# Idle-fill matmuls of TensorE in ten operand forms on a constant tile, instead of one bfloat16 form on the causal mask

## The chip, the cores and the metric

The kernel runs on one core of one Trainium2 chip. The metric is the device time of one execution in microseconds; lower is better. Times are the median over runs.

## The reference, cut to what matters

Two stages follow each other. The first is a linear recurrence with complex decay over 768 steps, for 4 batches and 8 heads of width 48; its output feeds a dense layer pair of width 384 to 2048 to 384 with a smooth gate.

```python
for t in range(S):                      # S = 768
    new_re = ar * S_re - ai * S_im      # decay a = a_re + i a_im, size limited to 0.999
    new_im = ar * S_im + ai * S_re
    S_re, S_im = new_re + k[t] x v[t], new_im
    y[t] = q[t] @ S_re
x = y as (3072, 384)
h = x @ w_in                            # 384 x 2048
g = h * tanh(softplus(h))
out = g @ w_out                         # 2048 x 384
```

The matmuls that this change is about are no part of it: their results are never read.

## The kernel before, in words

The 3072 rows are handled as 12 units of 256 steps, each in two chunks, a and b, of 128. Per unit, VectorE, ScalarE and GpSimd turn the decays into growth factors and phases (`elementwise`), DMAs relay the factors into a layout by heads (tile `T`), TensorE does the chunked recurrence (`attention`: `kn`, `am`, `y`, `pd`), DMAs move the result (`y` to `x`), and TensorE does the two dense layers (`moe`: `ph` and `po`). The weights arrive as 64-bit words and are joined on VectorE while unit 0 runs. From unit 1 on the dense layers split each float32 operand in a high and a low half of type float32r and issue three matmuls; unit 0 takes plain float32.

The order on each engine is written out by hand in the table `ORDER`, which lists operations by number; every engine runs its own operations in that order, and a semaphore wait holds all that stands behind it on the same engine. Before unit 0's recurrence can start, TensorE has little to do: it sums log magnitudes and phases along the steps by matmuls with triangular matrices (`sum_up`: `mag sum` and `phase sum`, with `turn` and `less` as the triangles), once for each chunk. Between these stand 40 operations called `spin` of two matmuls each, 80 in all, that write a PSUM tile `junk` which nobody reads. In TensorE's order they stand as follows: 12 spins (below: group A), phase sum of chunk a, 5 spins (B), mag sum a, 4 spins (C), mag sum b, 1 spin (D), phase sum b, 16 spins (E), the first recurrence matmuls of chunk a up to `pd`, 1 spin (F), `y` of chunk a and the sums of unit 1, 1 spin (G) between the `pkn` and `pa` matmuls of chunk b, and then the rest.

The spins read `cmask`, the 128x128 bfloat16 mask of the recurrence, as stationary operand and, repeated four times, as moving operand. GpSimd makes `cmask` and all other constants at the start: a memset and an affine select for `cmask`, five single columns (`halfpi` to `above`), `turn`, `less`, `identity`, `rmask`, `good` and `ones`. `good` is the tile into which VectorE's first operation (L452) adds up its checks, so that operation waits for its memset.

Sizes: `P` is 128, `TU` is 256, `WC` is 768, `SPIN` is 2. The tag `wp5` is the home of the split input weights of pair 5 (`wh`), which are first written long after the spins.

Of the kernel before, what the change touches and what calls it, by code (L numbers as in the profile page):

```python
# [13 lines left out]
F32 = mybir.dt.float32  # L14
BF16 = mybir.dt.bfloat16
F32R = mybir.dt.float32r
# [10 lines left out]
P = 128  # L27
TU = 256
# [7 lines left out]
WC = DM * DF // P // NPAIR  # L36
# [4 lines left out]
SPINS, SPIN = 40, 2  # L41
# [166 lines left out]
def tile_kernel(ctx, tc, q, k, v, are, aim, are_t, aim_t, w_in, w_out, out):  # L208
    nc = tc.nc
    const = ctx.enter_context(tc.tile_pool(name="const", bufs=1))  # L210
    wts = ctx.enter_context(tc.tile_pool(name="wts", bufs=1))
# [12 lines left out]
    cmask = const.tile([P, P], BF16, name="cmask")  # L224
# [2 lines left out]
        out=cmask, in_=cmask, compare_op=ALU.is_ge, fill=0.0, base=0,  # L227
        pattern=[[1, P]], channel_multiplier=-1,
    )
    halfpi = const.tile([P, 1], F32, name="halfpi")  # L230
    nc.gpsimd.memset(halfpi, math.pi / 2)
    tiny = const.tile([P, 1], F32, name="tiny")
# [8 lines left out]
    for n, x in (("turn", INV2PI), ("less", -2.0 * INV2PI)):  # L241
        sums[n] = const.tile([P, P], F32, name=n)
        nc.gpsimd.memset(sums[n], x)
        nc.gpsimd.affine_select(
            out=sums[n], in_=sums[n], compare_op=ALU.is_ge, fill=0.0, base=0,
            pattern=[[1, P]], channel_multiplier=-1,
        )
    identity = const.tile([P, P], F32, name="identity")
    make_identity(nc, identity)
    ident = identity[:2 * D, :2 * D]  # L250
# [473 lines left out]
    def moe(u, st, row0, op=op, act=act, po_tag="po", g_tag="g"):  # L724
# [74 lines left out]
        def store(t):  # L799
            return lambda e: e.dma_start(out[ds(row0 + t * P, P), :], o[t])  # L800
# [36 lines left out]
        for t in range(2):  # L837
            op("AV", f"u{u} o{t}", o_out(t))
            op("S", f"u{u} store{t}", store(t))

    junk = Tiles({"junk": (ps, "po", 2, [P, 512])})

    def spin(e):
        for _ in range(SPIN):
            e.matmul(junk["junk"], cmask, cmask.unsqueeze(1).broadcast_to([P, 4, P]), start=True, stop=True)

    def verdict():
        def tally(e):
# [22 lines left out]
    for u in range(UNITS):  # L871
        for _ in early[u]:
            pass
        if u == 0:
            for _ in range(SPINS):
                op("T", "spin", spin)
        attention(u, early[u + 1] if u + 1 < SUMMED else iter(()))
        if u == 0:
            for i in range(NW):
                weight(i)  # L880
        if u == 1:
            for i in range(NW):
                halves(i)
        if u + 1 == UNITS:
            for i in range(SUMMED):
                test(i)
            verdict()
        moe(u, units[u], u * TU)
# [126 lines left out]
def build(nc_run=True):  # L1015
    nc = _bacc.Bacc("TRN2", target_bir_lowering=False, num_devices=1, dynamic_dma_scratch_size=1024)
    F = NJ * TU
    aps = []
    for n in ("q", "k"):
        aps.append(nc.dram_tensor(n, (UNITS, P, F), F32, kind="ExternalInput").ap())  # L1020
    aps.append(nc.dram_tensor("v", (UNITS, P, NCH, DM), F32, kind="ExternalInput").ap())
    for n in ("a_re", "a_im"):
        aps.append(nc.dram_tensor(n, (UNITS, P, F), F32, kind="ExternalInput").ap())
    for n in ("a_re_t", "a_im_t"):
        aps.append(nc.dram_tensor(n, (SUMMED, P, F), F32, kind="ExternalInput").ap())
    for n in ("w_in", "w_out"):
        aps.append(nc.dram_tensor(n, (NPAIR, P, WC), I64, kind="ExternalInput").ap())
    out = nc.dram_tensor("out_0_dram", (B * S, DM), F32, kind="ExternalOutput").ap()
    with tile.TileContext(nc) as tc:
        tile_kernel(tc, *aps, out)  # L1030
    if not nc.is_finalized():
        nc.finalize()
    return nc
# [37 lines left out]
```

## Time and profile before

| | us |
|---|---|
| runs shown | 591.19 and 589.83 |
| median of them | 590.51 |
| span of the profiled execution, first to last instruction | 587.9 |
| median less span (what lies around it, and scatter) | 2.6 |
| TensorE matmul busy in the span | 579.2 (99%) |
| VectorE busy | 469.3 (80%) |
| ScalarE busy | 474.4 (81%) |
| GpSimd busy | 23.0 (4%) |

Of the profiled execution no time is given beside its span; the runs are timed without a profile and their median lies 2.6 us above the span. Times of rows are microseconds from the start of the span. In rows, PE is TensorE's matmul, PEld its loading of the stationary operand, DVE VectorE, ACT ScalarE, POOL GpSimd. Matmuls are pipelined, so a row's duration overlaps the next; the step from one start to the next is what a matmul costs in a stream. One float32 matmul leaves two records, one of bfloat16 or float32r one.

### The profile page before, as it was taken

The page shows a single profiled execution, that of the slowest core. Times are in us where ns is not written, and L with a number is a line of the kernel's source. Part 1 is how long each engine was busy: PE and PEld are TensorE (multiplying, and loading weights), DVE is VectorE, ACT ScalarE, POOL GpSimd, SP SyncE. Part 2 cuts the span into 40 slices and gives each one's busy share as a digit, 9 for nine tenths or more (in the row PEclk, how much of TensorE's full clock was granted, in tenths as well). Part 3 has the DMA queues.
Part 4 walks back from the last instruction along what each step waited for, and adds up shares of the span by engine and source line. Part 5 has one row for each costly group of instructions (what it writes and reads, how often), then busy time and mean ns, then how long its engine had stood idle before and what let it go on. Part 6 is the DMA issues. An engine that isn't in the chain of part 4 may idle for free.

```text
span 587.9 us, 11893 instructions
## 1 busy us (share of the span) xinstructions
PE 579.2 (99%) x4654; PEld 549.6 (93%) x4654; DVE 469.3 (80%) x830; ACT 474.4 (81%) x762; POOL 23.0 (4%) x37
## 2 busy tenths in 40 slices
PE   8999999999999999999999999999999999999996
PEld 4689887999999999999999999999999999999996
DVE  6999999999999889886779978878777855455453
ACT  8899999999997998789998769786974966555572
POOL 2010000101000100000001001001000000000000
PEclk9999999999999999999999999999999999999999
DMA  8788975413535352370181071261063043001000
GB/s 301 244 260 287 272 222 149 126 25 97 176 81 165 98 138 64 93 204 1 53 193 53 18 227 55 77 194 55 14 191 95 1 120 88 26 13 28 28 1 31
DMA packets 57167, 67.05 MB, mean 114 GB/s; under 512 B 4832, under 2 KB 50144, under 8 KB 57104
## 3 DMA queue, kind: packets, MB, share of 16 engines
q1 hardware_dynamic: 56320, 65.37, 37.9%
q8 instruction: 38, 0.62, 0.5%
q10 hardware_dynamic: 720, 0.66, 0.5%
q14 instruction: 25, 0.20, 0.1%
q0 software_dynamic: 64, 0.20, 0.1%
HBM read 37.75 MB, written 4.72 MB: 72 GB/s over the span
## 4 chain that ended last, share of the span: by engine, by line
PE 92%; ACT 2%; DMA 2%; DVE 2%; SPq 1%; POOL 0%; issue 0%; ACTq 0%; DVEq 0%; POOLq 0%
PE ph L746 36%; PE po L783 35%; PE pa L620 7%; PE ypsum L638 7%; PE pd L651 4%; PE pkn L608 2%; ACT X L172 1%; DMA x<-y 1%; DMA I<-a_im 1%; ACT L170 1%; SPq L552 1%; DVE w L291 0%; PE pd L668 0%; PE psum L404 0%; DVE am L627 0%
## 5 line engine op out<-in xcount | busy, mean ns | idle before, releaser
L172 ACT ACTIVATE e<-e 128x512 f32<-128x512 f32 x192 | 118.1, 627 | 31.8 <-DVE e L815 30.4
L746 PE MATMUL ph<-xH,wh 128*128 128x256 f32 x462 | 132.8, 288 | 0.0
L746 PE MATMUL ph<-xL,wh 128*128 128x256 f32 x462 | 129.7, 281 | 0.0
L746 PE MATMUL ph<-xH,wl 128*128 128x256 f32 x462 | 129.5, 280 | 0.0
L783 PE MATMUL po<-wh,gh 128*128 128x384 f32 x308 | 106.0, 344 | 0.0
L783 PE MATMUL po<-wh,gl 128*128 128x384 f32 x308 | 104.3, 338 | 0.0
L783 PE MATMUL po<-wl,gh 128*128 128x384 f32 x308 | 104.1, 338 | 0.0
L746 PEld LDWEIGHTS ph<-xH,wh 128*128 128x128 f32 x462 | 87.0, 188 | 0.9 <-issue 0.4
L746 PEld LDWEIGHTS ph<-xL,wh 128*128 128x128 f32 x462 | 87.0, 188 | 0.3
L746 PEld LDWEIGHTS ph<-xH,wl 128*128 128x128 f32 x462 | 87.0, 188 | 0.0
L759 DVE SCALAR_TENSOR_TENSOR g<-e,ph 128x512 f32<-128x512 f32 x96 | 65.3, 681 | 27.2 <-ACT e L172 26.7
L172 ACT ACTIVATE e<-ph 128x512 f32<-128x512 f32 x96 | 56.6, 590 | 36.5 <-PE ph L746 24.0
L771 DVE TENSOR_TENSOR gl<-g,gh 128x512 fp32r<-128x512 f32 x88 | 60.0, 685 | 17.0 <-ACT gh L765 10.6
L172 ACT ACTIVATE e<-e,fifth 128x512 f32<-128x512 f32 x96 | 68.8, 719 | 1.3
L815 DVE TENSOR_SCALAR e<-e 128x512 f32<-128x512 f32 x96 | 40.4, 424 | 26.9 <-ACT e L172 26.7
L783 PEld LDWEIGHTS po<-wh,gh 128*128 128x128 f32 x308 | 57.9, 188 | 0.2 <-issue 0.2
L783 PEld LDWEIGHTS po<-wh,gl 128*128 128x128 f32 x308 | 57.9, 188 | 0.1
L783 PEld LDWEIGHTS po<-wl,gh 128*128 128x128 f32 x308 | 57.8, 188 | 0.0
L170 ACT ACT_TABLE_LOAD x44 | 56.5, 1283 | 0.7
L620 PE MATMUL pa<-T 96*128 96x128 f32 x384 | 49.1, 277 | 0.9 <-DVE am L627 0.8
L620 PEld LDWEIGHTS pa<-T 96*128 96x128 f32 x384 | 46.0, 191 | 1.7 <-DVE am L627 1.0
L627 DVE TENSOR_TENSOR am<-pa,cmask 128x512 f32<-128x512 f32 x48 | 32.4, 684 | 4.9 <-PE pa L620 4.9
(136 smaller groups left out, 1053.1 us busy)
## 6 DMA issues: line engine op xcount, KB each, us to landing
T<-QK SPq DMA_DIRECT2D x70, 129.0 KB, 3.1
T<-X SPq DMA_DIRECT2D x69, 129.0 KB, 3.1
words<-w_in SPq DMA_DIRECT2D x8, 768.0 KB, 6.5
words<-w_out SPq DMA_DIRECT2D x8, 768.0 KB, 5.5
QK<-k SPq DMA_DIRECT2D x12, 384.0 KB, 4.5
QK<-q SPq DMA_DIRECT2D x12, 384.0 KB, 4.6
V<-v SPq DMA_DIRECT2D x12, 384.0 KB, 4.6
R<-a_re SPq DMA_DIRECT2D x12, 384.0 KB, 3.9
```

The lines of the kernel that those rows point to most:

```text
L170: self.nc.scalar.preload_act_table_set(need)
L172: return self.nc.scalar.activation(out, in_, func, **kw)
L608: e.transpose(d["pkn", g][:, i, :], T()[:, 4 * g + i, 1, :C], ident)
L620: e.matmul(d["pa", g][:, i, :], T()[:, 4 * g + i, 1, :C], T()[:, 4 * g + i, 0, :C], start=True, stop=True)
L627: e.tensor_tensor(d["am", g], d["pa", g], cmask.unsqueeze(1).broadcast_to([P, 4, C]), ALU.mult)
L638: e.matmul(ypsum[64 * par:64 * par + D, i, :], lhs, rhs, start=m == 0, stop=first or m == 1)
L651: e.matmul(d["pd", g][:, i, :], d["kn"][:, h, :], st["V"][:, c, h * D:(h + 1) * D], start=not held, stop=not held or i == 3)
L746: e.matmul(ph[k][:, slot(k, j, a), :], win(x, j, kt, a), st[y][:, kt, cols(k)], start=n == 0, stop=n + 1 == len(todo))
L759: e.scalar_tensor_tensor(g_[k], e_[k], 2.5, ph[k], ALU.subtract, ALU.mult)
L771: e.tensor_tensor(gs[k][1], g_[k], gs[k][0].bitcast(F32), ALU.subtract)
L783: e.matmul(po[t], x[:, slot(k, j, a), 0 if halved else t * P:C if halved else (t + 1) * P], wout(y, j, a), start=j == 0 and a == 0 and n == 0,
L815: op("V", f"{n} cap", lambda e, k=k: e.tensor_scalar_min(e_[k], e_[k], math.exp(20.0)))
```

## The change

A new float32 tile `idle` of 128 x 2 x 768, all 0.25, takes the place of `cmask` in the spins. It is filled by three memsets on GpSimd: its first 512 columns right behind `cmask`'s memset, the other 256 + 768 behind `less`. The spins count themselves, and number n takes form n mod 10, always two matmuls: float32r of 512 columns (form 0), the same with both matmuls in one accumulation group (1), float32r of 256 columns (2), of 512 columns taken from every second element (3), of a 128-column piece repeated four times (4), of one column repeated 512 times (5), bfloat16 of 512 columns (6), float32r over 64 of the 128 partitions (7), plain float32 of 512 columns (8), and float32r of 512 other columns (9). Number, place and destination of the spins stay; only their operands change.

```diff
+    idle = wts.tile([P, 2, WC], F32, tag="wp5", name="idle")
+    nc.gpsimd.memset(idle[:, 0, :512], 0.25)
     halfpi = const.tile([P, 1], F32, name="halfpi")
...
+    nc.gpsimd.memset(idle[:, 0, 512:], 0.25)
+    nc.gpsimd.memset(idle[:, 1], 0.25)
     identity = const.tile([P, P], F32, name="identity")
...
+    spun = [0]
     def spin(e):
-        for _ in range(SPIN):
-            e.matmul(junk["junk"], cmask, cmask.unsqueeze(1).broadcast_to([P, 4, P]), start=True, stop=True)
+        k = spun[0] % 10
+        spun[0] += 1
+        still, x, h = idle[:, 0, :P].bitcast(F32R), idle.rearrange("p a c -> p (a c)").bitcast(F32R), idle.rearrange("p a c -> p (a c)").bitcast(BF16)
+        y, z = junk["junk"], junk["junk"][:, :TU]
+        for n in range(SPIN):
+            if k == 0:
+                e.matmul(y, still, x[:, :512], start=True, stop=True)
+            elif k == 1:
+                e.matmul(y, still, x[:, :512], start=n == 0, stop=n + 1 == SPIN)
+            elif k == 2:
+                e.matmul(z, still, x[:, :TU], start=True, stop=True)
+            elif k == 3:
+                e.matmul(y, still, x[:, :1024].rearrange("p (a two) -> p a two", two=2)[:, :, 0], start=True, stop=True)
+            elif k == 4:
+                e.matmul(y.rearrange("p (a c) -> p a c", a=4), still, x[:, :P].unsqueeze(1).broadcast_to([P, 4, P]), start=True, stop=True)
+            elif k == 5:
+                e.matmul(y, still, x[:, :1].broadcast_to([P, 512]), start=True, stop=True)
+            elif k == 6:
+                e.matmul(y, h[:, :P], h[:, :512], start=True, stop=True)
+            elif k == 7:
+                e.matmul(y, still[:64], x[:64, :512], start=True, stop=True)
+            elif k == 8:
+                e.matmul(y, idle[:, 0, :P], idle[:, 1, :512], start=True, stop=True)
+            else:
+                e.matmul(y, still, x[:, 1024:1536], start=True, stop=True)
```

On GpSimd, before, the constants from `cmask` on stand in this order (rows give line, operation, what is written from what, and its size):

```order
L225 MEMSET cmask 128x128
L231 MEMSET halfpi 128x1
...
L239 MEMSET above 128x1
L243 MEMSET turn 128x128
L226 ISA
L226 AFFINE_SELECT cmask<-cmask 128x128
L244 AFFINE_SELECT turn<-turn 128x128
L243 MEMSET less 128x128
...
L252 MEMSET rmask 128x768
L255 MEMSET good 128x42
```

On GpSimd in the changed kernel the same stretch is this:

```order
L225 MEMSET cmask 128x128
L231 MEMSET idle 128x512
L226 ISA
L226 AFFINE_SELECT cmask<-cmask 128x128
...
L246 AFFINE_SELECT less<-less 128x128
L250 MEMSET idle 128x256
L251 MEMSET idle 128x768
masks.py:197 MEMSET identity 128x128
L256 MEMSET rmask 128x768
masks.py:199 AFFINE_SELECT identity<-identity 128x128
L257 MEMSET rmask 128x6
L259 MEMSET good 128x42
```

All three memsets of `idle` stand ahead of `good` there, and the small memset of `rmask` (six columns) has moved ahead of `good` as well.

On TensorE, before, the one spin between the first `pd` and the first `ypsum` matmuls of unit 0 (group F) is this:

```order
L620 MATMUL pa<-T 128x128 x8
L608 MATMUL pkn<-identity,T 128x96 x4
L651 MATMUL pd<-V,kn 96x48 x4
L845 LDWEIGHTS cmask
L845 MATMUL junk<-cmask 128x512
L638 MATMUL ypsum<-am,V 48x128 x8
```

On TensorE in the changed kernel, the end of group E and the same place with F (lines from L844 on are 28 higher, those ahead of it 4):

```order
L873 MATMUL junk<-idle 128x512 x2
L855 MATMUL junk<-idle 128x512 x2
...
L869 MATMUL junk<-idle 128x512 x2
L612 MATMUL pkn<-identity,T 128x96 x4
L624 MATMUL pa<-T 128x128 x8
...
L655 MATMUL pd<-V,kn 96x48 x4
L871 MATMUL junk<-idle 128x512 x2
L642 MATMUL ypsum<-am,V 48x128 x8
```

Nothing has moved on TensorE; the spin of group F has become form 8 (L871, plain float32), and the explicit weight loads of the bfloat16 matmuls are no longer rows of their own for the float32 forms.

## Rows read from the trace of the kernel before

**Rows 1.** The page's chain of work that ended last, by engine.

```profile
PE 92%; ACT 2%; DMA 2%; DVE 2%; SPq 1%; POOL 0%; issue 0%; ACTq 0%; DVEq 0%; POOLq 0%
```

**Rows 2.** Busy time by stretch: us, PE, PEld, DVE, ACT, POOL, PEclk, DMA.

```profile
0.00:42.00 42.00, 39.01 (x281) 27.03 (x282) 36.31 (x71) 37.13 (x64) 5.44 (x23) 1.00 0.83 275
42.00:583.00 541.00, 540.15 (x4375) 522.61 (x4373) 433.02 (x760) 436.78 (x698) 17.57 (x14) 1.00 0.36 102
```

**Rows 3.** TensorE's timeline, 0 to 45 us: start, us, what, [idle before].

```profile
1.72 6.75 PE L845 MATMUL junk<-cmask 128*128 128x512 bf16 x24 [1.72 <-POOL cmask L226]
8.30 0.83 PE L409 MATMUL psum<-turn,I 128*128 128x128 f32 x6
...
11.92 0.49 PE L404 MATMUL psum<-turn,X 128*128 128x128 f32 x2 [0.62 <-DVE X L478]
...
13.36 1.89 PE L845 MATMUL junk<-cmask 128*128 128x512 bf16 x8
...
16.85 0.38 PE L409 MATMUL psum<-turn,I 128*128 128x128 f32 x2
...
18.19 7.07 PE L845 MATMUL junk<-cmask 128*128 128x512 bf16 x32
25.10 0.49 PE L608 MATMUL pkn<-identity,T 96*128 96x96 f32 x4
...
28.01 0.85 PE L651 MATMUL pd<-V,kn 128*96 128x48 f32 x8 [0.28 <-DVE am L627]
28.70 0.59 PE L845 MATMUL junk<-cmask 128*128 128x512 bf16 x2
...
41.59 2.94 PE L746 MATMUL ph<-x,w 128*128 128x128 f32 x24 [0.30 <-DMA x<-y]
```

**Rows 4.** Timeline of TensorE's weight loads, one ahead of each spin matmul.

```profile
2.12 0.15 PEld L845 LDWEIGHTS <-cmask 128*128 128x128 bf16 x1 [0.28 <-issue]
2.55 0.15 PEld L845 LDWEIGHTS <-cmask 128*128 128x128 bf16 x1 [0.28 <-issue]
...
4.63 3.34 PEld L845 LDWEIGHTS <-cmask 128*128 128x128 bf16 x16 [0.23 <-issue]
```

**Rows 5.** TensorE's timeline in three dense stretches: float32, float32r 256, float32r 384.

```profile
47.72 5.52 PE L746 MATMUL ph<-x,w 128*128 128x128 f32 x48
53.08 2.75 PE L783 MATMUL po<-w,g 128*128 128x384 f32 x8
55.66 0.61 PE L746 MATMUL ph<-x,w 128*128 128x128 f32 x4
...
105.70 0.28 PE L746 MATMUL ph<-xH,wl 128*128 128x256 f32 x1
106.41 0.28 PE L746 MATMUL ph<-xH,wl 128*128 128x256 f32 x1
...
239.79 0.34 PE L783 MATMUL po<-wh,gl 128*128 128x384 f32 x1
243.33 0.34 PE L783 MATMUL po<-whl,gh 128*128 128x384 f32 x1
```

**Rows 6.** GpSimd's timeline, 0 to 4 us.

```profile
0.82 0.20 POOL L225 MEMSET cmask<- 128x128 bf16 x1 [0.29 <-POOLq L1016]
0.96 0.10 POOL L231 MEMSET halfpi<- 128x1 f32 x1
...
2.63 0.74 POOL L252 MEMSET rmask<- 128x768 uint8 x1
3.30 0.14 POOL L255 MEMSET good<- 128x42 f32 x1
```

**Rows 7.** VectorE's timeline, 3 to 12 us.

```profile
3.47 0.56 DVE L452 SCALAR_TENSOR_TENSOR X<-R 128x384 f32<-128x384 f32 x1 [1.98 <-POOL ones L867]
...
11.45 0.41 DVE L478 TENSOR_SCALAR X<-X 128x384 f32<-128x384 f32 x1
```

**Rows 8.** The chain of work that ended last, from 0 to 60 us.

```profile
3.48 0.57 DVE X L452 x2
...
8.39 3.89 ACT X L172 x8
```

## Prediction

> **What bounds the kernel now.** I read the chain of waits first: TensorE carries 92% of it, all other engines a few per cent together [rows 1]. The table by stretch says where: from 42 to 583 us TensorE is busy 540.15 of 541.00 us, up to 42 us it is busy 39.01 of 42.00 [rows 2]. From 42 us on it waits for next to nothing, so whatever delays the first dense-layer matmul, at 41.59 us [rows 3], delays the end by as much, and nothing later can take it back. The change touches only what lies ahead of that matmul. So the question is how much later than 41.59 us it starts.
>
> Ahead of it two chains run side by side. One is TensorE's own stream, in which the fills stand between real matmuls [rows 3]. The other is the elementwise work of unit 0: VectorE's first operation at 3.47 us, released by GpSimd's last memsets [rows 7], and then ScalarE, which alone holds the chain from 8.39 us for 3.89 us [rows 8]. They meet where TensorE sits idle for data: 0.62 us at 11.92 for VectorE, 0.28 us at 28.01 for VectorE, 0.30 us at 41.59 for the moved `x` [rows 3]. A longer fill costs nothing where such a wait follows, and its full length elsewhere.
>
> **Prices.** A bfloat16 fill of 512 columns costs 0.425 us at the start (2.12 to 2.55) and about 0.21 us later, 16 in 3.34 us [rows 4]; group E gives 0.216 (6.91 us, from 18.19 to 25.10, for 32) [rows 3]. That is 1.2 and then 2.4 columns per ns, the two levels of the clock, although the column of the granted clock reads 1.00 throughout [rows 2]. The step up comes near 4.6 us.
>
> Float32r: six steps of 256 columns take 0.71 us, 0.118 each; twenty of 384 take 3.54 us, 0.177 each [rows 5]. The straight line gives 0.236 for 512. Plain float32: 48 records of 128 columns from 47.72 to 53.08 are 0.112 each, 8 of 384 columns from 53.08 to 55.66 are 0.3225 each [rows 5]; the line gives 0.428 for a record of 512 columns. A matmul has two records, so 0.856. A spin of two matmuls therefore goes from 0.432 us to 0.472 (float32r, 512), 0.237 (form 2), 0.432 (form 6) or 1.712 us (form 8). Only form 8 is a large step: +1.28 us. It comes four times, once each in A, C, E and F.
>
> The Trainium skill, page "TensorE: Matmul & The Clock Gate", section "Back-to-back issue gap", gives columns/2.4 plus 2.5 ns for a matmul at the full clock. By that float32r would take 0.109, 0.162 and 0.216 us at 256, 384 and 512 columns; the rows show 0.118 and 0.177, so the measurement decides against it here. By the page the sum below would be +4.2 instead of +4.9 us.
>
> No row shows a float32r moving operand that strides (form 3) or stands still (form 5), nor one over 64 partitions (form 7). I take the contiguous price; the upper bound is twice that, the lower one the contiguous price itself, since no column goes in faster than a contiguous one in any row.
>
> **The change, group by group.**
>
> GpSimd: a memset of 128 elements takes 0.14 us (0.82 to 0.96), one of 768 takes 0.67 (2.63 to 3.30) [rows 6], so 0.035 + 0.00083 us per element. `idle` adds 512, 256 and 768 elements: 0.46 + 0.25 + 0.67 = 1.38 us, all queued ahead of `good`. VectorE's first operation waits for `good` and goes from 3.47 to about 4.87: +1.40. Behind it on VectorE stands the whole elementwise chain, and ScalarE, which runs on without a break, keeps the delay. The bounds are 0, if a transfer already holds that operation to the same time, and 1.5 us, with the `rmask` columns that also moved ahead.
>
> A (12 spins). The first fill waits for the first memset of `idle` instead of the select of `cmask` and starts near 1.55 instead of 1.72 us. At the low clock forms 0, 1, 2 and 3 take 0.85 + 0.85 + 0.43 + 0.85, to 4.54 us; form 3 wants the rest of the tile, ready near 3.6 by the prices above, when its turn is at 3.69. Form 4 has one slow and one fast matmul (0.66); then 0.47, 0.43, 0.47, 1.71, 0.47, 0.47, 0.47 bring A to 9.70. Phase sum a ends at 10.37; VectorE reads it right ahead of L478 (11.45 [rows 7]), so after the delay at about 12.4. Hidden.
>
> B (forms 2 to 6) is 0.237 + 3 x 0.472 + 0.432 = 2.08 us, to 12.45. Mag sum a wants L478's result, 11.86 + 1.40 = 13.26: TensorE still waits, and the chain is late by the +1.40 alone.
>
> C (7, 8, 9, 0): 3 x 0.472 + 1.712 = 3.13 against 8 x 0.215 = 1.72: +1.41, not hidden, since mag sum b has its data long before (its X is 1.4 us later, the fills end 2.8 later). D (form 1): +0.04. Phase sum b starts at 16.85 + 2.85 = 19.7 [rows 3], and VectorE's read of it is some 2.4 us late, still less than what follows on TensorE.
>
> E (forms 2 to 9, then 0 to 7): 2 x 0.237 + 11 x 0.472 + 2 x 0.432 + 1.712 = 8.24 against 6.91: +1.33. At 25.10 the kernel before goes from fill to `pkn` without idle time [rows 3], so the relayed tile was there; its relay is late by 1.4, TensorE by 4.2. In full.
>
> F is one spin of form 8: +1.28. The idle 0.28 us at 28.01 just ahead of it goes, since TensorE is later than VectorE by then: -0.28. G (form 9): +0.04. The idle 0.30 us at 41.59 [rows 3] goes too, as the move of `x` depends on `y` of chunk a, which is late by as much as TensorE, less its own slack: -0.30.
>
> Sum: 1.40 + 1.41 + 0.04 + 1.33 - 0.28 + 1.28 + 0.04 - 0.30 = +4.9 us. The first dense matmul moves from 41.59 to 46.5, the span from 587.9 to 592.8, and the time, 2.6 us above the span as before, from 590.5 to 595.4 us.
>
> **Rivals.**
>
> *Striding or standing operands cost double.* In E forms 3 and 5 come twice each; one of them at double price adds 4 x 0.236 = 0.94 us, both 1.9: 596.3 to 597.3. In B they only fill the wait ahead of 13.26. For it: no row shows these forms. Against: phase sum b, of whose six matmuls every other one (L411) reads one column 128 times, takes 1.34 us from 16.85 to 18.19 [rows 3], 0.112 for each of its 12 records, the contiguous price of [rows 5]. The Trainium skill, page "SBUF — State Buffer", section "Door 1: The DMA port swizzle", says that reads keep full speed as long as two fall into the same 16 bytes, which a step of two float32 does; no run here shows it yet.
>
> *GpSimd's delay is hidden.* If the first decays land only when `good` is done, B's end decides: 12.45 against 11.92, +0.53 instead of +1.40, 594.5. For it: no row shows when they land. Against: the trace puts the wait down to GpSimd [rows 7], and 1.4 us is long.
>
> *The float32 form does not do what it says* and runs as one record like the others: C +0.17, E +0.09, F +0.04, G and D as above; +1.2 in all, 591.7. Against: float32 matmuls of the dense layer leave two records at 0.3225 [rows 5].
>
> *Slower: the new fills do not count as activity, and the clock stays at 1.2 GHz until the recurrence.* Then A ends near 13.9, B near 19.1, so mag sum a is 7.2 instead of 1.4 us late (+5.8); the three sums of 12 records cost double (3 x 1.34, +4.0), C 5.95 instead of 3.13 (+2.8), E 15.3 instead of 8.2 (+7.1): about +20 on top of the forecast, 615. It decides from the point where a fill after 5 us still steps by more than 0.42. Against: float32r and float32 hold 2.4 columns per ns, or near, from 47 us on [rows 5]. A clock that rises seven fills later is a small case of it: A is 7 x 0.21 = 1.5 us longer, and as B then ends at 13.95 instead of 12.45, 0.6 of it is seen beyond 13.32, where mag sum a starts anyway: 596.0.
>
> The Trainium skill, "TensorE: Matmul & The Clock Gate", section "What's actually happening", says that the throttled state is the default and that activity releases it; by that rule, this rival is what happens if a form does not count. The trace agrees as far as it goes, with fills that step at 0.425 and then at 0.21 us.
>
> **How the numbers follow.** Forecast 595.4: 0.62. Double price: 0.15. Hidden delay: 0.10. Late clock: 0.04. One-record float32: 0.05. Clock down through E: 0.04. The runs shown lie 0.7 us on either side of their median, which I add to the bounds. The range of 592.5 to 598.5 us holds the first four and leaves out the last two. Two per cent, about what a measurement of this kernel can tell from no change, is 11.8 us, so 602.3 and 578.7: slower 0.04, within 0.95, faster 0.01.
>
> **What would show it.** VectorE's first operation near 4.87 us; junk steps of 0.236 us in float32r and of two records of 0.43 in form 8; mag sum a near 13.3, the first `pkn` near 29.3 and the first `ph` near 46.5 us, without idle time ahead of it; from there on the same rows as before, 4.9 us later. The prediction is wrong if the first `ph` moves by less than 2 or more than 8 us, if fills still step at the low clock after 5 us, or if TensorE waits anew behind it.

## The result, and the profile after

The changed kernel takes 597.93 us (597.25 and 598.62) against 590.51 (589.83 to 591.19): ratio 1.0133, 95% interval 1.0102 to 1.0165, or +7.4 us. A second measurement of 6 runs gave 598.29 against 591.10, ratio 1.0116 (1.0095 to 1.0137), +7.2. That is within 2% and inside the range of 592.5 to 598.5, 2.5 us above the forecast of 595.4.

The profiled execution of the changed kernel is one of its two runs (598.62 us, span 596.9), so the profiled runs are timed too; in the thirteen whose time is on record it lies 1.7 to 1.8 us above the span, so some 0.9 of the 2.6 us given for the kernel before is scatter, by estimate. It splits as before. Busy time by stretch, columns as in [rows 2]:

```profile
50.00:591.00 541.00, 539.83 (x4370) 522.02 (x4368) 433.03 (x760) 437.05 (x698) 17.40 (x14) 1.00 0.36 102
```

After the first dense matmul TensorE is again all but always busy. The change is in what lies ahead. TensorE's timeline of the changed kernel, columns as in [rows 3]:

```profile
5.65 1.06 PE L865 MATMUL junk<-idle 128*128 128x512 f32 x2
6.50 1.08 PE L867 MATMUL junk<-idle 128*128 128x512 bf16 x2
7.51 0.85 PE L869 MATMUL junk<-idle 64*128 64x512 f32 x2
...
11.49 0.83 PE L413 MATMUL psum<-turn,I 128*128 128x128 f32 x6
...
14.21 0.60 PE L867 MATMUL junk<-idle 128*128 128x512 bf16 x2
14.65 0.38 PE L408 MATMUL psum<-turn,X 128*128 128x128 f32 x2
...
15.77 0.39 PE L408 MATMUL psum<-less,X 128*128 128x128 f32 x2
16.09 0.73 PE L869 MATMUL junk<-idle 64*128 64x512 f32 x2
...
19.50 0.38 PE L408 MATMUL psum<-turn,X 128*128 128x128 f32 x2
...
21.30 0.38 PE L413 MATMUL psum<-turn,I 128*128 128x128 f32 x2
...
22.88 1.07 PE L861 MATMUL junk<-idle 128*128 128x512 f32 x2
23.77 0.65 PE L863 MATMUL junk<-idle 128*128 128x512 f32 x2
24.26 0.60 PE L865 MATMUL junk<-idle 128*128 128x512 f32 x2
24.70 0.60 PE L867 MATMUL junk<-idle 128*128 128x512 bf16 x2
25.23 0.73 PE L869 MATMUL junk<-idle 64*128 64x512 f32 x2
25.90 1.98 PE L871 MATMUL junk<-idle 128*128 128x512 f32 x4
...
32.33 0.55 PE L612 MATMUL pkn<-identity,T 96*128 96x96 f32 x4
...
34.86 0.80 PE L655 MATMUL pd<-V,kn 128*96 128x48 f32 x8
...
37.38 1.08 PE L642 MATMUL ypsum<-am,V 128*48 128x128 f32 x16
...
49.03 2.91 PE L750 MATMUL ph<-x,w 128*128 128x128 f32 x24
```

The reader is to see the steps from start to start. Fills still step by about 0.43 us a matmul until about 7.7 us: the pair of form 5 (L865) takes 0.85 us from 5.65 to 6.50, and 0.44 from 24.26 to 24.70. Mag sum a (14.65) has no idle time ahead of it, where it had 0.62 us before. Form 3 (L861) takes 0.89 us a pair in group E, form 7 (L869) 0.67. The first `ph` starts at 49.03 instead of 41.59: +7.44 us, which is the measured difference.

GpSimd's last memset and VectorE's first operation in the changed kernel, timelines, to be held against [rows 6, 7]:

```profile
4.74 0.13 POOL L259 MEMSET good<- 128x42 f32 x1
```

```profile
4.91 0.56 DVE L456 SCALAR_TENSOR_TENSOR X<-R 128x384 f32<-128x384 f32 x1 [3.42 <-POOL ones L895]
```

VectorE's first operation is at 4.91 us (forecast 4.87).

### The profile page after: what moved, and what is told of

Read it like the earlier page. It is cut to its first block, busy times and chain, and to the rows that moved or that the text cites. A ratio compares the mean times of both kernels' runs of the same rounds, so it can differ in the third digit from the quotient of the medians.

```text
span 596.9 us, 11910 instructions
## 1 busy us (share of the span) xinstructions
PE 588.3 (99%) x4662; PEld 557.4 (93%) x4662; DVE 469.7 (79%) x830; ACT 475.0 (80%) x762; POOL 23.6 (4%) x40
## 4 chain that ended last, share of the span: by engine, by line
PE 94%; ACT 4%; DMA 0%; issue 0%; DVE 0%; SPq 0%; POOL 0%; ACTq 0%; POOLq 0%
PE po L787 34%; PE ph L750 33%; PE pa L624 7%; PE ypsum L642 7%; PE pd L655 5%; PE pkn L612 2%; PE junk L871 1%; ACT X L172 1%; ACT L170 1%; ACT e L172 1%; PE junk L861 1%; PE junk L869 0%; PE psum L408 0%; PE junk L855 0%; ACT words L172 0%; DMA x<-y 0%
```

## The experiments

The theory after the result: most of the forecast's terms hold, and three things made it 2.5 us too low, namely a clock that stepped up near 7.7 instead of 4.6 us, the strided form at half pace, and dearer steps at form 7, into it and within it. The rivals are stated with each run. Differences are to the kernel before, run beside it on the same chip; a few tenths of a per cent of scatter remain in a median (the kernel before ran from 588.1 to 594.0 us), so the start of the first `ph`, 41.59 us before and 49.03 after, is given too.

**GpSimd's memsets alone** (pool_only), on the kernel before:

```diff
+    idle = wts.tile([P, 2, WC], F32, tag="wp5", name="idle")
+    nc.gpsimd.memset(idle[:, 0, :512], 0.25)
...
+    nc.gpsimd.memset(idle[:, 0, 512:], 0.25)
+    nc.gpsimd.memset(idle[:, 1], 0.25)
```

> The kernel before with the three memsets of the new tile added on GpSimd, which no matmul reads; the fills stay bfloat16 on the mask. Theory (a memset ahead of the check tile delays VectorE's first operation, and the whole elementwise chain with it, by 1.4 us, which TensorE's cheap fills leave visible): VectorE's first operation at 4.9 us, mag sum a at 13.3, first dense matmul near 43.0, time 1.4 us above the kernel before. Rival (the delay is made up for by idle time before the first dense matmul): less than 0.5 us above it.

592.14 against 590.92 us, ratio 1.0017 (0.9997 to 1.0036), +1.2. VectorE's first operation at 4.92 us, first `ph` at 43.02. TensorE's timeline of this kernel:

```profile
29.47 0.85 PE L655 MATMUL pd<-V,kn 128*96 128x48 f32 x8 [0.29 <-DVE am L631]
...
43.02 2.94 PE L750 MATMUL ph<-x,w 128*128 128x128 f32 x24 [0.29 <-DMA x<-y]
```

The waits stand as before, 1.43 to 1.46 us later: the theory holds in the trace, and the time agrees without being settled by itself.

**The tile filled by VectorE** (dve_fill), on the changed kernel:

```diff
-    nc.gpsimd.memset(idle[:, 0, :512], 0.25)
+    nc.vector.memset(idle[:, 0, :512], 0.25)
```

and the same for the other two memsets.

> The changed kernel with the new tile filled by VectorE, idle at that time, instead of GpSimd. Theory (with the slow start of the clock TensorE's fills in A and B end at 14.65 us, later than the data at 13.3, so GpSimd's delay is no longer what counts): VectorE's first operation back at 3.5 us, mag sum a still near 14.6, time as the changed kernel within 0.4 us, 7.4 above the kernel before. Rival (each delay adds up): 1.4 us less, 6.0 above.

597.88 against 590.92 us, ratio 1.0103 (1.0062 to 1.0144), +7.0. VectorE is back at 3.47 us, but the first `ph` is at 48.83, only 0.20 earlier. TensorE's timeline:

```profile
3.84 1.09 PE L861 MATMUL junk<-idle 128*128 128x512 f32 x2
4.75 1.03 PE L863 MATMUL junk<-idle 128*128 128x512 f32 x2
...
6.44 1.08 PE L867 MATMUL junk<-idle 128*128 128x512 bf16 x2
7.45 0.73 PE L869 MATMUL junk<-idle 64*128 64x512 f32 x2
...
14.02 0.60 PE L867 MATMUL junk<-idle 128*128 128x512 bf16 x2
14.46 0.38 PE L408 MATMUL psum<-turn,X 128*128 128x128 f32 x2
```

Mag sum a (14.46) follows the fills of B at once; its data were there 1.4 us earlier (VectorE's L482 runs from 12.65 to 13.07 us). In an execution with a late clock GpSimd's delay is covered by the fills. Both delays do not add up.

**Form 3 made contiguous** (no_stride), on the changed kernel:

```diff
         k = spun[0] % 10
+        k = 0 if k == 3 else k
```

> The changed kernel with form 3 (every second element) replaced by form 0 (contiguous). Theory (a float32r operand of stride two goes in at half pace, 0.44 instead of 0.236 us a matmul): B shorter by 0.4, E by 0.8 us, time 1.2 to 1.4 us below the changed kernel, 6.1 above the one before. Rival (the long steps of form 3 belong to the switch from 256 columns to 512): no difference, 7.4 above.

597.47 against 590.92 us, ratio 1.0101 (1.0060 to 1.0141), +6.6. First `ph` at 47.46, 1.57 earlier than in the changed kernel. TensorE's timeline, the start of E:

```profile
21.87 0.49 PE L860 MATMUL junk<-idle 128*128 128x256 f32 x2
22.19 0.62 PE L856 MATMUL junk<-idle 128*128 128x512 f32 x2
22.65 0.62 PE L864 MATMUL junk<-idle 128*128 128x512 f32 x2
```

The pair in place of form 3 takes 0.46 us instead of 0.89, in the same place behind form 2. So the long step belongs to the stride, not to the switch. The trace shows this; the time, 6.6 above with an interval that reaches 8.3, would fit the rival's 7.4 as well.

**Form 8 made float32r** (no_f32), on the changed kernel:

```diff
         k = spun[0] % 10
+        k = 0 if k == 8 else k
```

> The changed kernel with form 8 (plain float32) replaced by form 0 (float32r). Theory (the four spins of form 8 in A, C, E and F each cost 1.24 us more, none of it hidden): 4.9 us below the changed kernel, 2.5 above the one before. Rival (A and C have slack against the elementwise chain, so only E and F count): 2.5 us below the changed kernel, 4.9 above the one before.

594.35 against 590.92 us, ratio 1.0052 (1.0030 to 1.0073), +3.4; first `ph` at 44.06, 4.97 earlier than in the changed kernel. TensorE's timeline:

```profile
4.83 0.74 PE L864 MATMUL junk<-idle 128*128 128x512 f32 x2
5.41 0.60 PE L866 MATMUL junk<-idle 128*128 128x512 f32 x2
5.84 0.60 PE L868 MATMUL junk<-idle 128*128 128x512 bf16 x2
```

The 4.97 us look like the theory's 4.9, but by luck. Here the fills are fast from 4.9 us on, although up to 7 us the program is that of the changed kernel. So a part of the 4.97 us was the clock's, and the last runs below take that up. The time, 3.4 above, lies between the theory's 2.5 and the rival's 4.9; its interval, 1.8 to 4.3, holds only the first.

**All fills bfloat16, or all float32r** (all_bf16, all_f32r), on the changed kernel, with `k = 6` and with `k = 0` for every spin:

```diff
         k = spun[0] % 10
+        k = 6
```

> The changed kernel with all fills in form 6 (bfloat16 on the constant tile). Theory (bfloat16 costs the same on constants as on the mask, so only GpSimd's delay is left): mag sum a at 13.3, first dense matmul near 43.0, 1.4 us above the kernel before, as the kernel with GpSimd's memsets alone; and the fills step up to the fast pace at any point between 4.5 and 8 us, as with the mask. Rival (constant operands keep the clock down longer): slow fills until 7.5 us or later and 2 us or more above.

591.55 against 590.89 us, ratio 1.0003 (0.9987 to 1.0019), +0.7.

> The changed kernel with all fills in form 0 (float32r, contiguous, 512 columns). Theory (0.23 to 0.236 us a matmul): C +0.17, E +0.5 to +0.6, F and G +0.04 each, with GpSimd's +1.4 and the two waits given back, first dense matmul near 43.3 us, 1.7 us above the kernel before. Rival (what E costs above the forms' own steps is a price of float32r fills): E longer by over 1 us, 2.5 us above or more.

592.40 against 590.89 us, ratio 1.0016 (0.9992 to 1.0039), +1.5. The float32r time fits its theory; the bfloat16 time, whose interval ends at 1.1 above, lies under the 1.4 expected, and its rival's 2 lies further off. Yet the first `ph` is at 43.99 and 44.16 us, later than expected. The profiled bfloat16 execution is the slowest of its ten (594.23 us), so what delayed it need not be in the others. TensorE's timeline, the float32r kernel:

```profile
19.72 7.55 PE L856 MATMUL junk<-idle 128*128 128x512 f32 x32
27.11 0.49 PE L612 MATMUL pkn<-identity,T 96*128 96x96 f32 x4
...
40.05 0.57 PE L672 MATMUL pd<-S,identity 96*96 96x192 f32 x2 [1.50 <-DVE am L631]
```

E takes 7.39 us for 32, 0.231 a matmul, against 6.91 for bfloat16: the forecast price of float32r. The rest is a wait of 1.50 us (1.34 with bfloat16) for VectorE, which in the bfloat16 kernel stood still for a weight transfer first. The timelines of VectorE and GpSimd there, and of GpSimd in the kernel with the memsets alone:

```profile
37.69 1.53 DVE L283 TENSOR_SCALAR words<-words 128x768 int32<-128x768 uint32 x1 [0.37 <-DMA words<-w_out]
```

```profile
37.26 1.54 POOL L469 TENSOR_TENSOR X<-X 128x768 f32<-128x768 f32 x1 [20.75 <-ACT X L172]
```

```profile
37.26 1.94 POOL L469 TENSOR_TENSOR X<-X 128x768 f32<-128x768 f32 x1 [20.74 <-ACT X L172]
```

VectorE's operation takes 1.53 us here and 0.55 in the kernel with the memsets alone. The traces point to the GpSimd operation beside it. Where GpSimd's starts first, as here, VectorE's ends 0.42 us behind it (39.22 against 38.80; 39.40 against 38.98 in the float32r kernel); with the memsets alone VectorE's starts first, at 37.25, and it is GpSimd's that is longer, 1.94 instead of 1.54 us. So the one seems to hold the other up, and a late weight transfer decides which; no run changes their order by itself. The fast pace began near 4.2 (bfloat16) and 5.1 us (float32r), so constants do not hold the clock down.

**A as before** (a_as_before), on the changed kernel:

```diff
+            if spun[0] <= 12:
+                e.matmul(y, cmask, cmask.unsqueeze(1).broadcast_to([P, 4, P]), start=True, stop=True)
-            if k == 0:
+            elif k == 0:
```

> The changed kernel whose first 12 spins (A) are the old ones, bfloat16 on the mask; B to G as changed. Theory (A with the form 8 spin and a late clock pushes B past the data at 13.3 us): A ends near 8.9 us, B near 12.1, mag sum a at 13.3 instead of 14.65, first dense matmul near 47.7, 1.3 us below the changed kernel, 6.1 above the one before. Rival (A is hidden, as the prediction had it): as the changed kernel, 7.4 above.

597.01 against 590.89 us, ratio 1.0101 (1.0079 to 1.0122), +6.1; first `ph` at 47.83, 1.20 earlier than in the changed kernel. TensorE's timeline:

```profile
8.76 0.83 PE L413 MATMUL psum<-turn,I 128*128 128x128 f32 x6
...
13.36 0.49 PE L408 MATMUL psum<-turn,X 128*128 128x128 f32 x2 [1.28 <-DVE X L482]
```

With A done at 8.76 instead of 11.49, TensorE waits for the data at mag sum a again, as the theory has it. But the clock stepped up near 5.3 us here, and the changed kernel with an early clock reaches the same 47.83 with A unchanged (after_look below). So this run does not tell the fills of A from the clock.

**No fills at all** (no_fill), on the kernel before:

```diff
-SPINS, SPIN = 40, 2
+SPINS, SPIN = 40, 0
```

> The kernel before with all 40 spins empty, so that TensorE only does its real work. Theory (the fills keep the clock up for the recurrence of unit 0; without them its first 3 to 6 us from 25 us on run at 1.2 GHz): the records of the first pkn and pa step by 0.22 us instead of 0.11, first dense matmul 1.5 to 3 us later than at 41.6, time 1.5 to 3 us above the kernel before. Rival (the elementwise chain alone sets that time): less than 0.5 us above. A second rival (the clock stays down until the dense layers): 8 us or more above.

594.20 against 590.89 us, ratio 1.0058 (1.0033 to 1.0083), +3.3; first `ph` at 45.67, 4.08 later than before. TensorE's timeline, then the busy time by stretch (the column before the last two is the granted clock):

```profile
18.87 0.39 PE L411 MATMUL psum<-turn,I 128*128 128x128 f32 x2
19.09 0.39 PE L409 MATMUL psum<-turn,I 128*128 128x128 f32 x2
...
24.72 0.72 PE L608 MATMUL pkn<-identity,T 96*128 96x96 f32 x4 [4.57 <-DMA T<-X]
25.23 3.68 PE L620 MATMUL pa<-T 96*128 96x128 f32 x16
...
37.99 0.63 PE L409 MATMUL psum<-turn,I 128*128 128x128 f32 x2
38.41 0.46 PE L414 MATMUL psum<-ncar,identity 128*128 128x128 f32 x2
```

```profile
24.00:38.00 14.00, 13.00 (x73) 12.30 (x74) 12.67 (x23) 9.36 (x17) 0.00 (x0) 0.53 0.81 270
```

Just before the wait of 4.57 us the phase sum still steps at the fast pace, 0.11 us a record (18.87 to 19.09 is two); behind it the 16 records of `pa` take 3.47 us instead of 1.81, and the low pace lasts to about 38.4 us, longer than the 3 to 6 us expected. The fills are worth 3 to 4 us; the changed ones give back twice that, so the changed kernel is slower than one without fills.

**The changed kernel twice more, and no_f32 once more** (after_again, after_look, no_f32_look), no new edit.

> The changed kernel once more. Theory (the time at which the clock steps up differs from execution to execution of one program, since a kernel with the same fills up to 7 us stepped up at 4.9 us and this one at 7.6): slow fills end anywhere from 4.2 to 8 us; mag sum a at 13.3 to 14.7, first dense matmul at 47.7 to 49.1 us, time 6.1 to 7.5 above the kernel before. Rival (these forms hold the clock down): slow fills until 7.4 us or later again.

> The changed kernel a third time, one look, for the same question: by the theory the step of the clock may come anywhere from 4.2 to 8 us, by the rival at 7.4 us or later.

> The changed kernel with form 0 in place of form 8 once more, one look. Theory (the step differs between executions): not tied to the 4.9 us of the first look. Rival (the kernel fixes it): 4.9 us again within 0.3.

In after_again the fast pace began near 7.7 us and the first `ph` was at 49.02 (this execution 597.42 us; the median is given above). In after_look it began near 4.9 and the first `ph` was at 47.83 (595.46 us). In no_f32_look it began near 5.9 instead of 4.9, and the first `ph` was at 44.07 (593.66 us). TensorE's timeline of after_look:

```profile
4.83 0.66 PE L863 MATMUL junk<-idle 128*128 128x512 f32 x2
5.33 0.59 PE L865 MATMUL junk<-idle 128*128 128x512 f32 x2
...
12.88 0.60 PE L867 MATMUL junk<-idle 128*128 128x512 bf16 x2
13.36 0.49 PE L408 MATMUL psum<-turn,X 128*128 128x128 f32 x2
```

One and the same program gets its fast clock at 4.9 or at 7.7 us, and its first `ph` moves by 1.19 us with it. The rival that these forms hold the clock down falls: after_look ran the same forms.

**The check tile first** (good_first), on the kernel before: the tile and memset of `good` moved up behind `cmask`'s memset.

```diff
+    good = const.tile([P, UNITS + SPLIT_UNITS, 3], F32, name="good")
+    nc.gpsimd.memset(good, 0.0)
     halfpi = const.tile([P, 1], F32, name="halfpi")
```

> The kernel before with the memset of the check tile moved up to second place on GpSimd. It asks whether VectorE's first operation waits for GpSimd or for its data. Theory (the data land shortly before GpSimd is done): VectorE starts 0.1 to 0.5 us earlier than 3.47 us, the first dense matmul as much earlier, the time equal to the kernel before within what a run can tell. Rival (the data are late): starts at 3.47 us again.

590.24 against 591.10 us, ratio 0.9995 (0.9975 to 1.0015). VectorE's timeline, then TensorE's:

```profile
3.35 0.56 DVE L452 SCALAR_TENSOR_TENSOR X<-R 128x384 f32<-128x384 f32 x1 [1.86 <-DMA R<-a_re_t]
```

```profile
41.59 2.94 PE L746 MATMUL ph<-x,w 128*128 128x128 f32 x24 [0.34 <-DMA x<-y]
```

The first operation moved by 0.12 us, as the theory has it, and the first `ph` not at all, against it; it waits for the move of `x`. The data land near 3.3 us, so nearly all of GpSimd's 1.4 us was a real delay. No run beats the kernel before by more than its measurement tells.

## Why the prediction was right, and where its sum was off

The frame of the prediction stood: the dense part was not touched, and the time moved by what the first `ph` moved. But one of its own signs of being wrong came true: in two of three profiled executions of the changed kernel fills still stepped at the low clock after 5 us. And 597.93 lies inside the range partly by luck: the late clock and the double price, held as rivals of their own, both came, and by the prediction's own prices the two together make 596.9 (595.4 + 0.6 + 0.94). The second measurement, 598.29, is inside only because the bound stands at 598.5, where those terms give 598.0 (597.3 + 0.7). Term by term, from the starts of the real matmuls in [rows 3] and in the changed kernel's timeline above:

| step | forecast us | measured us |
|---|---|---|
| mag sum a | +1.40 | +2.73 (14.65 - 11.92) |
| C, with mag sum a | +1.41 | +1.69 (4.85 against 3.16, to mag sum b) |
| D | +0.04 | +0.03 |
| E, with phase sum b | +1.33 | +2.78 (11.03 against 8.25) |
| first `pkn` to `pd` | -0.28 | -0.38 |
| F, `pd` to `ypsum` | +1.28 | +1.30 (2.52 against 1.22) |
| `ypsum` to `ph`, with G | -0.26 | -0.71 (11.65 against 12.36) |
| sum | +4.92 | +7.44 |

Two starts in the kernel before, from the same view as [rows 3]:

```profile
15.08 0.39 PE L404 MATMUL psum<-turn,X 128*128 128x128 f32 x2
...
29.23 1.08 PE L638 MATMUL ypsum<-am,V 128*48 128x128 f32 x16
```

The two waits given back are worth more than their idle times of 0.28 and 0.30 us, since the rows overlap; the one ahead of `ph` is worth 0.47, by the step from the last `pd` row to `ph` (39.80 to 41.59 before, 47.71 to 49.03 after).

*Mag sum a.* The step that did not hold is "TensorE still waits": the forecast had B end at 12.45, 0.8 us ahead of the data. GpSimd's term by itself is right (4.91 us, pool_only +1.43). But with the clock stepping up near 7.7 us A ended at 11.49 instead of 9.70, and B, with form 3 at double price, at 14.65. Even with an early clock (after_look) A ended at 10.16 and B at about 13.32, by form 6 from 12.88 at 0.44 us, where VectorE's data (L482) were ready at 13.31. So mag sum a at 13.36 there, +1.44, agrees with the forecast's +1.40 by a coincidence: the fills alone would have brought it to about the same place. The forecast held the late clock for a case of 0.04 that adds 0.6 us; it adds 1.2 (after_look against the other two profiles of the same program), because form 3 and a longer A had already used up the slack. Two of three profiles of the changed kernel were late, which does not look like 0.04.

*E and C.* Form 3 takes 0.89 us a pair, near the rival's double price of 0.94; making it contiguous took 1.57 us off the first `ph`, with the clock late in both. At the low clock it costs hardly more than the others: 0.91 us a pair in dve_fill (3.84 to 4.75) against 0.85 for a contiguous one. So it takes about 0.45 us a matmul at either clock, and it is the high clock that it does not profit from. Form 5, one column read 512 times, takes 0.44 and is the cheapest of the 512-column float32r forms by 0.02. The Trainium skill, page "SBUF — State Buffer", section "Door 1: The DMA port swizzle", says that a step of two float32 costs nothing; for this operand the trace does not agree, 0.445 against 0.23 us a matmul at the high clock. What is left of E (2.78 - 1.33 = 1.45, of which 0.84 is form 3 twice) lies, but for small differences either way, at form 7, twice: its pair takes 0.67 instead of 0.47, and the row ahead of it is 0.10 longer. That row is form 6 in E, 0.53, but form 6 ahead of mag sum a takes 0.44 (14.21 to 14.65), so this is not the price of bfloat16; in C it is a mag sum matmul, 0.32 (15.77 to 16.09) instead of 0.22. About the same 0.3 us is what C costs over its forecast (1.69 against 1.41). Whether it belongs to 64 partitions as such was not tried: no run leaves form 7 out and keeps the rest.

*Form 8* cost what two records of 0.43 make: F grew by 1.30 us. no_f32 has its first `ph` 4.97 us earlier, where four times 1.24 would be 4.96, but 1.2 of that was the clock's: with the clock at 4.9 us in both (after_look, 47.83) the gap is 3.8, three times 1.24. Without form 8 TensorE waits 1.05 us at mag sum a, so in such an execution the one in A is hidden, as the forecast had it.

*Rivals.* Double price held for the stride and fell for the standing column. The hidden delay of GpSimd fell as a mechanism of transfers (good_first), but its other half, that B's end decides, holds in executions with a late clock (dve_fill). The one-record float32 and the clock kept down through E fell: E steps at the high pace throughout. The argument against the last, that float32 too holds 2.4 columns per ns from 47 us on, misread [rows 5]: 128 columns in 0.112 us are 1.14 for each record. What tells the clock of a float32 record is its own step, 0.11 us here against 0.21 in the slow stretch of no_fill.

*The rest.* From the first `ph` to the end of the time, 547.6 to 550.2 us pass in the thirteen profiled executions whose own time is known, whichever kernel. This scatter, whose cause is not shown, is why the spans differ by 9.0 us and the medians by 7.4, and why times alone could not settle terms of a microsecond; the starts in the traces could.

## What to carry to other kernels

A fill on an in-order engine is free only up to the moment at which the real work behind it is ready, so it is to be sized by its longest form at the slow clock, not by its count. Constants for it are work too: where the engine that makes them also makes something the first real operation waits for, they go behind that. Price operand forms from rows of the same form, and where the trace has none, keep double for anything that strides. Two rivals that push the same way should be added up too, not only taken one at a time.

## What the runs showed of the hardware

- The pace of the fills stepped up to that of 2.4 GHz at 4.2 to 7.7 us in the profiled executions of kernels with fills, for the same program at 4.9 and at 7.7. The column of the granted clock reads 1.00 in the first microseconds, while matmuls step at the pace of 1.2 GHz (0.43 us for 512 columns); the steps show it, the column does not.
- Without fills TensorE's float32 records of 128 columns stepped by 0.21 us from 12.4 to 17.5 us and by 0.11 from 18.8 to 19.9. Then it stood idle, 4.57 us by its row, and stepped by 0.21 again from about 25 to 38.4 us, busy 13.00 of the 14.00 us from 24 to 38; there the column showed it (0.53). What ended the slow stretch was not tried.
- A float32r moving operand of every second element goes in at 0.445 us for 512 columns at the high clock and at about 0.45 at the low one; contiguous takes 0.23 and 0.43, one column repeated 0.22 at the high clock.
- Where a GpSimd operation and a VectorE operation of 128x768 each met, the one that started second took longer: 1.94 instead of 1.54 us on GpSimd, 1.53 instead of 0.55 us on VectorE. That each waits for the other is read from the order of their rows, not shown by a run.
